# Threshold attention and a squared-ReLU layer: new PSUM homes and step orders in attention, and four weight chunks converted in the first layer

## The chip, the core and the metric

The kernel runs on one core of one Trainium2 chip. The metric is device time in microseconds: the median of several executions. A profile shows one execution, instruction by instruction.

The core's engines each run their own queue in order: TensorE (PE in the profile; PEld is its loading of weights), VectorE (DVE), ScalarE (ACT), GpSimd (POOL) and SyncE (SP), which here issues nearly all DMAs. PE writes its results to PSUM, which has eight banks of 512 fp32 columns; DVE and ACT read them there.

## The reference

```python
def _attn_ref(q, k, v, tau):                      # q, k, v: (8, 8, 576, 64), float32
    scale = 1.0 / np.sqrt(q.shape[-1])
    scores = scale * np.matmul(q, k.transpose(0, 1, 3, 2))
    thresh = np.max(scores, axis=-1, keepdims=True) - tau
    scores = np.where(scores >= thresh, scores, -1000000000.0)
    scores = scores - np.max(scores, axis=-1, keepdims=True)
    attn = np.exp(scores)
    attn = attn / (np.sum(attn, axis=-1, keepdims=True) + 1e-09)
    return np.matmul(attn, v).astype(np.float32)

def _moe_ref(x, w_in, w_out):                     # x: (4608, 512); w_in: (512, 2048); w_out: (2048, 512)
    h = np.maximum(x @ w_in, 0.0)
    return (h * h @ w_out).astype(np.float32)
```

The attention's output, put back to (batch, position, head and channel), is x. The weights w_in and w_out come as 64-bit floats; the kernel converts them to 32-bit floats itself.

## The kernel before

**Three stages.** Attention comes first and writes x, transposed, to DRAM. The first layer (`hidden_layer`, L837, products at L849) and the second (`output_layer`, L955, products at L984) follow, each in nine steps of 512 tokens. Both layers save products with a fast matrix scheme of two levels: each step forms 49 products from sums of operand blocks, so sums of weight blocks must be made on the way (`sums`, L251).

**Units and periods.** Attention works on two heads of a batch at once. A unit is 128 queries of such a pair against all 576 keys (four units a pair, and one that joins the last 64 queries of two pairs): 144 units. A period (`period`, L624) handles two units, A and B, and there are 72 periods, with a few before and after to fill and empty the pipeline. The steps of a period, by their names in the order lists:

- `SA`, `SB` (`scores`, L427, product L438): scores of A and of B. A's lie in banks 0 and 5, B's in 2 and 3, and the last 64 keys of both in parts of banks 1 and 4.
- `topA0` ... `topB1` (L455): DVE copies the scores of one head to SBUF and finds their smallest negated value, which is the maximum.
- `powA0` ... (L466): ACT's exponentials. `leastA`, `leastB` (L463): GpSimd adds tau to the thresholds. `maskA0` ... (L471): DVE applies the mask and sums.
- `over` (L478, GpSimd) and `inv` (L481, DVE): the reciprocal of the sums; `spread` (`widen`, L514) lays it out wide on GpSimd.
- `U`, `V`, `W` (`fill`, L503, `half_turn`, L377, L381): PE turns the masked weights of a period, 8, 8 and 2 blocks (W with the two blocks of the spread reciprocals). `eU`, `eV`, `eW` (`filled`, L523, L528): ACT copies them to SBUF.
- `PV` (`values`, L530, L537): 72 products of weights and values. `x` (L651): DVE and ACT take the result out; `xs` (L666): GpSimd scales the half that ACT took and SP sends x to DRAM (`ask`, L581).
- `T`, `eT` (`turn`, L392, L399): PE turns the next queries or keys, ACT takes them out (L406, L414), and the next loads are issued (`load_q` L291, `load_k` L301).
- `c1` ... `c6` (L200 to L247): the conversion of one weight chunk of 128x512, on ACT (`c1`, `c2`), GpSimd (`c3`, `c6`) and DVE (`c4`, `c5`). `fetch` (L178) loads a chunk on SP. `s1` (`sums_step`, L575): one sum of first-layer weight blocks on GpSimd, in periods without a chunk.

**PSUM homes before.** `sc` holds banks 0 to 5, `pt` the other two as one buffer of two banks. U and V both use pt, one after the other; W uses banks 2 and 3; PV uses banks 0 and 5; T uses 1 and 4.

**What sets the order.** The order is written out by hand. Each list (`PLAIN`, `CONVERTING`, `FIRSTS` for the first periods, L599 to L616) names the steps of a period; the program issues them in that order, and each engine executes its share in that order. Which unit a step works on is fixed in the table `steps` (L695): scores, maxima, exponentials, masks of this period; U and PV of two periods ago; V and W of the period before. `touch` (L356) adds the waits between engines that meet in a bank.

**Chunks.** There are 32 chunks: 16 of w_in and 16 of w_out. `EARLY = 16` (L164) is the number of w_out chunks converted in attention; chunk m begins in period m + 2 (L567). `convert_out` (L1082) can convert half chunks within steps of the first layer, four a step (`PER`, L1121); with 16 early chunks it has none to do.

Of the kernel before, what the change touches and what calls it, by code (L numbers as in the profile page):

```python
# [48 lines left out]
def kernel(  # L49
# [114 lines left out]
    EARLY = 16  # L164
# [136 lines left out]
    def load_k(i):  # L301
# [4 lines left out]
        for j in range(2):  # L306
# [10 lines left out]
            queue.dma_start(out=rn[REST:P, ds(j * D, D)], in_=keys[:, CH - 1, :])  # L317
        queue = nc.sync if i else nc.scalar
        queue.dma_start(
            out=rn[0:REST, :].rearrange("p (j d) -> p j d", j=2),  # L320
            in_=q[b, h : h + 2, MAIN:S, :].rearrange("j p d -> p j d"),
        )
# [31 lines left out]
    MEET = (("q scores", "turned q", (Q_RING,)), ("scores", "turned k", (K_RING,)), ("q scores", "turned k", (K_RING,)), ("values", "weights", (W_RING,)), ("x", "weights", (W_RING,)))  # L354
# [22 lines left out]
    def half_turn(pt, slot, of, at=None):  # L377

        for r in range(2):
            rows = ds(r * HALF, HALF)  # L380
            made = nc.tensor.transpose(pt[:, r, ts(slot, HALF)], of[rows, :], ident[rows, rows])  # L381
            touch("turns", made, at and at + r * BANK, BANK)

    def whole(pt, slot, count):

        return pt[:, :, ds(slot * HALF, count * HALF)].rearrange("p r (t q) -> p r t q", q=HALF)
# [5 lines left out]
    def turn(i, which, spots, other=None):  # L392
# [15 lines left out]
        def then():  # L408
            part = lambda r, x, n: (spots[r][0][:, ds(x, n)], spots[r][1])
            if which:  # L410
                for r, n in ((0, half), (1, half + REST)):
                    spot = part(r, 0, n)
                    copy_by = other if r and other else nc.scalar.copy
                    touch(kind, copy_by(to[1][:, ds(r * half, n)], spot[0]), spot[1], BANK, i)  # L414
                scaled(to[2], part(0, half, REST))
                next_keys(i)
            else:
                for r in range(2):
                    scaled(to[0][:, ds(r * half, half)], part(r, 0, half))
# [83 lines left out]
    def fill(m, f, pt, at=None):  # L503
# [19 lines left out]
    def filled(m, f, pt, at=None):  # L523
# [3 lines left out]
        to = wT[m][:, ds(weight_at(first) * P, count * P)]  # L527
        touch("weights", nc.scalar.copy(joined(to), whole(pt, 0, count)), at, 2 * BANK, m)  # L528

    def values(m):  # L530

        for c in range(CH):
            for u in range(2):
                for s, (i, _, count, row) in enumerate(halves(2 * m + u)):
                    for j in range(2):
                        rows = ds(j * D, D)
                        made = nc.tensor.matmul(  # L537
                            sc[ds(u * D, D), ds(5 * j * BANK + row, count)], loaded_v[i][rows, (c - (u != j)) % CH, :],
# [3 lines left out]
                        touch("values", made, 5 * j * BANK, BANK, m)  # L542
# [47 lines left out]
    def converts(p):  # L590
        return is_wide and (has_chunk(p) or has_chunk(p - 1))
# [4 lines left out]
    def begun(n):  # L596
# [3 lines left out]
        fetch U SA topA1 over s1 topA0 SB topB1 inv sV eU powA1 V topB0 leastA spread PV powA0 maskA1 leastB maskA0 eV T powB1 x maskB1 powB0 xs maskB0 eT W eW  # L600
    """.split()
    CONVERTING = """
        fetch c1 T SA topA1 c3 topA0 U eU powA1 SB topB0 over topB1 powA0 c4 powB0 PV eT inv leastA maskA1 x powB1 leastB spread V eV maskA0 W maskB0 c5 c6 eW maskB1 xs c2
# [4 lines left out]
            SA SB id4 fetch topA1 topA0 powA1 leastA powA0 topB1 T id14 powB1 topB0 powB0 eT maskA0 leastB maskA1 maskB1 maskB0  # L608
        """.split(),
        1: """  # L610
            SA topA1 SB topA0 id4 topB0 over inv powA1 V eV spread T powA0 topB1 eT W id4 leastA maskA1 leastB powB1 maskA0 maskB1 powB0 maskB0 fetch eW
        """.split(),
        2: """
            T SA fetch c2 U topA1 c3 over eU SB powA1 topA0 c4 powA0 c5 topB0 powB0 leastA topB1 eT maskA1 PV inv powB1 V leastB x spread maskA0 eV maskB1 maskB0 W eW xs c6 c1
        """.split(),
    }  # L616

# [6 lines left out]
    def period(p):  # L624

        A, B_, a, b = 2 * p, 2 * p + 1, 2 * p - 2, 2 * p - 1
        m, turns = p - 2, TURNS.get(p, ())
        late, pt = {"W": []}, {}

        def fills(f, m):  # L630
            if has(2 * m):
                pt[f] = pt_pool.tile([P, 2, BANK], FP32, tag="pt", name="pt")
                fill(m, f, pt[f])

        def evict(f, m):
            if has(2 * m):
                filled(m, f, pt[f], 2 * BANK if f == "W" else None)

        def W():
            if has(2 * m + 2):  # L640
                pt["W"] = middle()
                fill(m + 1, "W", pt["W"], 2 * BANK)

        def turn_some():
            late["turn"] = [turn(g // 2, g % 2, spots()) for g in turns]

        def PV():
            if has(2 * m):
                values(m)

        def given_out():  # L651
            if has(2 * m):
                x = sb.tile([P, 2, P], FP32, tag="x", bufs=2, name="x")
                by_vector = (0,)
                for j in range(2):
                    by = sc[:, ds(5 * j * BANK, P)], wT[m][:, ts(SCALE_AT + j, P)]
                    if j in by_vector:
                        made = nc.vector.tensor_tensor(out=x[:, j, :], in0=by[0], in1=by[1], op=ALU.mult)  # L658
                    else:
                        made = nc.scalar.copy(x[:, j, :], by[0])  # L660
                    touch("x", made, 5 * j * BANK, P, m)
                late["x"] = x, [j for j in range(2) if j not in by_vector], wT[m]
                wT.pop(m)
                valued(m)
# [588 lines left out]
```

## Time and profile before

| | us |
|---|---|
| median of 3 runs | 1290.56 (1289.38 to 1292.22) |
| the profiled execution | 1292.2 |
| its span, first to last instruction | 1290.4 |
| PE busy | 1261.3 |
| DVE busy | 998.5 |
| ACT busy | 854.9 |
| POOL busy | 897.4 |

An engine's busy time joins its records, and records of one engine can overlap, since an instruction is begun before the one ahead of it has ended; the cost of an instruction in a full queue is then the time from its start to the next start. A row of the order in time gives start, length, engine, line, operation, out<-in, shape and count, and in brackets the idle time ahead of it with what ended that. A row of waits gives who waited for whom, the sum, how often, and the longest. A row of stretches gives the window, its length and the busy time of PE, PEld, DVE, ACT and POOL.

### The profile page before, as it was taken

The numbers are of one execution on the slowest core, as the hardware profiler recorded it, in microseconds if no ns is written. First come the engines' busy times: TensorE is split into PE (matmuls) and PEld (weight loads), VectorE is DVE, ScalarE is ACT, GpSimd is POOL, SyncE is SP. The second block draws the span as 40 slices with busy tenths as digits, with TensorE's granted clock in tenths as the row PEclk, the third lists the DMA queues.
The fourth block names the chain that finished last, engine by engine and source line by source line (L and its number), as shares of the span: only waits on it lengthen the run. The fifth ranks groups of instructions, "written<-read, shape, count | busy, mean of one in ns | idle before, by whom it ended". The sixth has DMA issues, their size and how long they took to land.

```text
span 1290.4 us, 46352 instructions
## 1 busy us (share of the span) xinstructions
PE 1261.3 (98%) x18627; PEld 1127.2 (87%) x18627; DVE 998.5 (77%) x2433; ACT 854.9 (66%) x1536; POOL 897.4 (70%) x1094
## 2 busy tenths in 40 slices
PE   8999998999999999999999999999999999999998
PEld 6666666677777768999999999999999999999998
DVE  6999999899999997787788778777745654665463
ACT  6999999899999995756675667566523432343240
POOL 2565565555555557888898789768777867776775
PEclk9999999999999999999999999999999999999999
DMA  5555666544333422556655665589545314522411
GB/s 149 157 149 152 162 189 182 140 94 115 88 83 83 103 48 67 180 169 205 204 185 177 212 199 178 176 322 394 188 148 164 113 57 160 165 90 79 160 34 34
DMA packets 247032, 192.05 MB, mean 149 GB/s; under 512 B 97184, under 2 KB 195488, under 8 KB 246816
## 3 DMA queue, kind: packets, MB, share of 16 engines
q1 hardware_dynamic: 245360, 188.63, 48.7%
q8 instruction: 147, 2.41, 0.8%
q10 hardware_dynamic: 1456, 0.44, 0.1%
q14 instruction: 69, 0.57, 0.1%
HBM read 116.65 MB, written 72.35 MB: 146 GB/s over the span
## 4 chain that ended last, share of the span: by engine, by line
PE 64%; DMA 2%; DVE 1%; ACT 1%; issue 0%; POOL 0%; SPq 0%; ACTq 0%; DVEq 0%; POOLq 0%
PE ph L849 30%; PE po L984 29%; PE sc L537 2%; PE sc L438 2%; DMA wall<-w 1%; PE pt L381 1%; DMA g<-arena 0%; PE sc L381 0%; PE sc L399 0%; DVE arena L456 0%; ACT c L795 0%; ACT arena L528 0%; DVE arena L125 0%; DVE arena L122 0%; POOL arena L125 0%
## 5 line engine op out<-in xcount | busy, mean ns | idle before, releaser
L125 POOL TENSOR_TENSOR arena<-arena 128x512 f32<-128x512 f32 (+1 forms) x314 | 378.1, 1224 | 108.7 <-DVE arena L125 92.0
L984 PE MATMUL po<-wall,arena 128*128 128x128 f32 x3528 | 394.7, 275 | 1.4 <-ACT arena L761 1.4
L984 PEld LDWEIGHTS po<-wall,arena 128*128 128x128 f32 x3528 | 394.3, 192 | 1.8 <-ACT arena L761 1.8
L849 PE MATMUL ph<-arena,wall 128*128 128x128 f32 x3528 | 394.4, 275 | 0.5 <-DVE arena L658 0.5
L849 PEld LDWEIGHTS ph<-arena,wall 128*128 128x128 f32 x3528 | 394.1, 192 | 0.7 <-ACT arena L660 0.6
L125 DVE TENSOR_TENSOR arena<-ph,arena 128x512 f32<-128x512 f32 x378 | 256.1, 688 | 86.9 <-PE ph L849 62.6
L122 POOL TENSOR_TENSOR arena<-arena 128x128 f32<-128x128 f32 (+2 forms) x314 | 255.2, 814 | 54.5 <-DMA arena<-w 36.7
L125 DVE TENSOR_TENSOR arena<-po,arena 128x128 f32<-128x128 f32 x378 | 108.2, 289 | 168.4 <-PE po L984 164.3
L466 ACT ACTIVATE arena<-arena 128x576 f32<-128x576 f32 x288 | 224.3, 858 | 16.7 <-DVE arena L456 16.7
L471 DVE SCALAR_TENSOR_TENSOR arena<-arena 128x576 f32<-128x576 f32 x288 | 225.7, 812 | 0.4 <-POOL arena L463 0.3
L456 DVE TENSOR_SCALAR_CACHE_REDUCE arena<-sc 128x576 f32<-128x576 f32 x288 | 204.2, 750 | 18.0 <-ACT arena L528 6.8
L795 ACT COPY c<-arena 128x512 f32<-128x512 f32 (+1 forms) x303 | 173.5, 579 | 49.5 <-DVE arena L122 41.5
L537 PEld LDWEIGHTS sc<-arena 64*64 64x64 f32 x5760 | 144.8, 133 | 44.3 <-DVE arena L456 40.4
L122 DVE TENSOR_TENSOR arena<-arena,c 128x512 f32<-128x512 f32 (+1 forms) x267 | 174.6, 662 | 5.8 <-ACT c L795 4.0
L438 PE MATMUL sc<-arena 64*64 64x64 f32 (+1 forms) x2304 | 170.6, 417 | 0.3 <-DVE arena L658 0.2
L537 PE MATMUL sc<-arena 64*64 64x128 f32 (+1 forms) x5760 | 160.6, 262 | 9.9 <-DVE arena L456 7.8
L528 ACT COPY arena<-pt 128x1024 f32<-128x1024 f32 x144 | 157.4, 1093 | 3.6 <-PE pt L381 3.6
L761 ACT COPY arena<-po 128x128 f32<-128x128 f32 x63 | 16.6, 264 | 186.8 <-PE po L984 184.0
L381 PEld LDWEIGHTS pt<-ident,arena 64*128 64x128 f32 x2304 | 83.3, 139 | 42.7 <-ACT arena L528 35.3
L761 ACT COPY arena<-ph 128x512 f32<-128x512 f32 x63 | 36.6, 581 | 121.8 <-PE ph L849 121.2
L381 PE MATMUL pt<-ident,arena 64*128 64x64 f32 x2304 | 101.0, 228 | 3.7 <-ACT arena L528 3.5
L438 PEld LDWEIGHTS sc<-arena 64*64 64x64 f32 x2304 | 62.8, 133 | 47.0 <-issue 22.6
(51 smaller groups left out, 941.4 us busy)
## 6 DMA issues: line engine op xcount, KB each, us to landing
g<-arena SPq DMA_DIRECT2D x144, 256.0 KB, 2.8
arena<-g SPq DMA_DIRECT2D x144, 256.0 KB, 4.2
w<-arena SPq DMA_DIRECT2D x60, 256.0 KB, 2.5
wall<-w SPq DMA_DIRECT2D x49, 256.0 KB, 5.3
arena<-w SPq DMA_DIRECT2D x44, 256.0 KB, 3.1
arena<-in_v_dram SPq DMA_DIRECT2D x32, 288.0 KB, 3.6
out_dram<-arena SPq DMA_DIRECT2D x70, 128.0 KB, 2.5
arena<-in_q_dram SPq DMA_DIRECT2D x64, 128.0 KB, 3.8
```

Source lines behind the costliest of these rows:

```text
L122: e.tensor_tensor(out=out, in0=x, in1=y, op=ALU.subtract)
L125: e.tensor_tensor(out=out, in0=x, in1=y, op=ALU.add)
L381: made = nc.tensor.transpose(pt[:, r, ts(slot, HALF)], of[rows, :], ident[rows, rows])
L438: made = nc.tensor.matmul(sc[at, ds(to, count)], lhs, kT[rows, ds(at_k, count)], start=True, stop=True)
L456: made = nc.vector.tensor_scalar(out=s[:, j, :], in0=sc[:, ds(at, S)], scalar1=1.0, scalar2=None, op0=ALU.mult, op1=ALU.min, accum_out=nmx ...
L466: nc.scalar.activation(out=w[:, :, j, :], in_=of(j), func=AF.Exp, bias=nmx[:, j : j + 1], scale=-1.0)
L471: nc.vector.scalar_tensor_tensor(out=w[:, :, j, :], in0=of(j), scalar=thr[:, j : j + 1], in1=w[:, :, j, :], op0=ALU.is_le, op1=ALU.mult, a ...
L528: touch("weights", nc.scalar.copy(joined(to), whole(pt, 0, count)), at, 2 * BANK, m)
L537: made = nc.tensor.matmul(sc[ds(u * D, D), ds(5 * j * BANK + row, count)], loaded_v[i][rows, (c - (u != j)) % CH, :], wT[m][rows, ds(weigh ...
L795: nc.scalar.copy(c, y)
L849: nc.tensor.matmul(to[:, j, :], W_IN[m, k][:, ts(j, P)], of[k][:, m - 1, :], start=(not more and j == 0), stop=True, skip_group_check=True,)
L984: nc.tensor.matmul(to, g[:, j, :], w[:, j, :], start=(not more and j == 0), stop=(j == 3), skip_group_check=True)
```

## The change

Five things change.

1. PSUM homes. V now goes to banks 2 and 3, W to banks 0 and 5, and PV to a tile of its own in pt (named `px`); U stays in pt. W's copy to SBUF becomes two copies, one a bank. `x` reads px.
2. Orders. All lists are new. A step may carry a lag, the number of periods that its unit lies back (`eV@2`: V of two periods ago); default lags stand in `LAGS`. In the plain order the period begins with smallest, exponential B1, masks of the period before, and PE runs U, T, SA, SB, PV, W, V. In the converting order PE runs SA, U, SB, PV, W, T, V, and U is of the period before.
3. `EARLY` is 12: the last four chunks of w_out leave attention, and `convert_out` converts them as eight half chunks in steps 0 and 1 of the first layer. A period counts as converting until two periods after the last chunk's beginning.
4. `load_k` loads the last keys of both heads with one DMA rather than two, all on SP's queue.
5. When queries or keys are taken out, the half in bank 4 goes first.

```diff
-    EARLY = 16
+    EARLY = 12
...
-            queue.dma_start(out=rn[REST:P, ds(j * D, D)], in_=keys[:, CH - 1, :])
...
+        last = k[b, h : h + 2, :, :].rearrange("j (p c) d -> p c j d", c=CH)[:, CH - 1, :, :]
+        nc.sync.dma_start(out=both(ds(REST, REST)), in_=last)
...
-        touch("weights", nc.scalar.copy(joined(to), whole(pt, 0, count)), at, 2 * BANK, m)
+        to = joined(wT[m][:, ds(weight_at(first) * P, count * P)])
+        if f == "W":
+            for r in (1, 0):
+                of = pt[r][:, ds(0, count * HALF)].rearrange("p (t q) -> p t q", q=HALF)
+                touch("weights", nc.scalar.copy(to[:, r, :, :], of), at[r], BANK, m)
+            return
...
     PLAIN = """
-        fetch U SA topA1 over s1 topA0 SB topB1 inv sV eU powA1 V topB0 leastA spread PV powA0 maskA1 leastB maskA0 eV T powB1 x maskB1 powB0 xs maskB0 eT W eW
+        fetch leastA@1 eW@2 U leastB@1 maskA0@1 maskB0@1 maskA1@1 powB1@1 maskB1@1 eV@2 T SA topA0 over inv sV s1 eU eT xs@3 SB topA1 spread topB0 powA0 PV topB1 powA1 powB0 W x V
...
     CONVERTING = """
-        fetch c1 T SA topA1 c3 topA0 U eU powA1 SB topB0 over topB1 powA0 c4 powB0 PV eT inv leastA maskA1 x powB1 leastB spread V eV maskA0 W maskB0 c5 c6 eW maskB1 xs c2
+        fetch over SA c5 eV@2 c1 c6 topA1 U@1 topA0 leastA eU@1 powA1 inv SB xs@3 PV powA0 spread topB0 maskA1 W powB0 topB1 maskA0 T c3@0 c2 powB1 eW x c4@0 leastB maskB1 V eT maskB0
...
+    LAGS = dict(
+        U=2, V=1, W=1, eU=2, eV=1, eW=1, PV=2, x=2, xs=2, over=1, inv=1, spread=1, c3=1, c4=1, c5=1, c6=1,
+    )
...
+        if f == "U":
+            late[f, m] = pt_pool.tile([P, 2, BANK], FP32, tag="pt", name="pt")
...
+        elif f == "V":
+            late[f, m] = middle()
...
+        else:
+            late[f, m] = [sc[:, ds(b * BANK, BANK)] for b in (0, 5)]
...
+            late["PV", m] = pt_pool.tile([P, 2, BANK], FP32, tag="pt", name="px")
```

More of the change, by code (lines that the diff above doesn't have):

```diff
@@ L410, in then @@
             if which:
-                for r, n in ((0, half), (1, half + REST)):
+                for r, n in ((1, half + REST), (0, half)):
                     spot = part(r, 0, n)
@@ L590, in converts @@
     def converts(p):
-        return is_wide and (has_chunk(p) or has_chunk(p - 1))
+        return is_wide and any(has_chunk(p - i) for i in range(3))
     def has_chunk(p):
@@ new lines, in evict, with turn_some, evict_turned, values_of @@
+    def evict(f, m):
+        if has(2 * m):
+            filled(m, f, late.pop((f, m)), {"U": None, "V": 2 * BANK, "W": (0, 5 * BANK)}[f])
+    def turn_some(p):
+        late["turn", p] = [turn(g // 2, g % 2, spots()) for g in TURNS.get(p, ())]
+    def evict_turned(p):
+        for then in late.pop(("turn", p)):
+            then()
+    def values_of(m):
+        if has(2 * m):
+            late["PV", m] = pt_pool.tile([P, 2, BANK], FP32, tag="pt", name="px")
+            values(m, late["PV", m])
```

193 lines of the change are left out of this document (88 added, 105 removed).

## The prediction

> **What bounds the kernel now.** I read the page first, then the busy time in stretches, then the order in time on TensorE (PE), ScalarE (ACT) and GpSimd (POOL), and last who waits for whom. All times are in one profiled execution.
>
> ```profile
> span 1290.4 us, 46352 instructions
> ```
> ```profile
> 133.00:217.00 84.00, 78.26 (x1939) 55.68 (x1942) 82.54 (x241) 84.00 (x149) 50.81 (x84) 1.00 0.68 186
> 217.00:256.00 39.00, 34.03 (x800) 24.30 (x800) 36.05 (x104) 35.80 (x61) 21.27 (x36) 0.96 0.54 147
> 256.00:482.00 226.00, 224.84 (x5754) 162.67 (x5752) 216.60 (x647) 214.50 (x363) 126.82 (x218) 1.00 0.38 88
> ```
> The columns are PE, PEld, DVE, ACT, POOL busy, then the granted clock, DMA share and GB/s. Attention has three stretches. While weight chunks are converted, ACT is busy 84.00 of 84.00 and DVE 82.54, so ACT sets the pace. From 256 us, without chunks, PE is busy 224.84 of 226. Between them lies a stretch in which no engine is full and the granted clock falls to 0.96. The first scores of a period (L438, "x24" or more) mark its start; four of them give the pace:
>
> ```profile
> 34.24 1.32 PE L438 MATMUL sc<-arena 64*64 64x512 f32 x24
> ```
> ```profile
> 216.88 1.32 PE L438 MATMUL sc<-arena 64*64 64x512 f32 x24
> ```
> ```profile
> 256.12 2.18 PE L438 MATMUL sc<-arena 64*64 64x512 f32 x32
> ```
> ```profile
> 481.79 2.18 PE L438 MATMUL sc<-arena 64*64 64x512 f32 x32
> ```
> They begin periods 4, 30, 35 and 71. So 26 converting periods take 182.64 us, 7.02 each; periods 30 to 34 take 39.24, 7.85 each; 36 plain ones take 225.67, 6.27 each. After attention PE hardly waits, so time is to be had in attention alone.
>
> What ends last in a plain period shows on three engines:
>
> ```profile
> 393.69 0.66 PE L381 MATMUL pt<-ident,arena 64*128 64x64 f32 x16
> 394.28 2.32 PE L438 MATMUL sc<-arena 64*64 64x512 f32 x32
> 396.53 0.72 PE L381 MATMUL pt<-ident,arena 64*128 64x64 f32 x16
> 397.24 2.19 PE L537 MATMUL sc<-arena 64*64 64x128 f32 x72
> 399.37 0.47 PE L399 MATMUL sc<-ident,arena 64*128 64x64 f32 x8
> ...
> 400.51 1.88 PE L438 MATMUL sc<-arena 64*64 64x512 f32 x28
> ```
> ```profile
> 395.32 1.05 ACT L528 COPY arena<-pt 128x1024 f32<-128x1024 f32 x1
> ```
> ```profile
> 396.43 0.75 DVE L456 TENSOR_SCALAR_CACHE_REDUCE arena<-sc 128x576 f32<-128x576 f32 x1
> ```
> ```profile
> PEld pt L381 <- ACT arena L528: 23.5, 29, 0.8
> ```
> PE's second turning (step V, 396.53) starts when ACT's copy of U ends at 396.37, since both use the pair of banks pt. The values (PV, 397.24) start when DVE's second maximum ends at 397.18, since PV writes banks 0 and 5, where the scores lie that DVE is reading. The loop "scores, two maxima, PV, three turnings, scores" is the 6.23 us from 394.28 to 400.51. The weight loads of the turnings waited 23.5 us on that copy in 29 periods, mostly under running products.
>
> **New homes and the plain order.** After the change PV has pt to itself once U is copied out; V goes to banks 2 and 3, W to 0 and 5. So PV no longer waits for maxima, and V no longer for U's copy. PE's order becomes U, T, SA, SB, PV, W, V, and DVE begins with the four masks of the period before. What is late next? PE's own work, start to start in the rows above: U 0.59; the scores 2.25 less the wait of some 0.1 before V; V some 0.55; PV 2.13; 399.37 to 400.51 for T, W and U, of which U is counted, leaves 0.55. That is 5.97. DVE, busy 216.60 of 226, needs 6.01 of its 6.27. ACT closes a loop from PV to PV: PV 2.13, W 0.45 to its end, 0.09 to ACT, W's copies 0.51, an exponential 0.67, V's copy 0.90, U's 1.05 and 0.16 to PE, 5.96 (the ACT durations from the rows of the next part). The change adds two waits: the scores SA (banks 0 and 5) wait for W's copies, SB (2 and 3) for V's, and all of PE's queue stands behind them; in this loop both copies are done some 0.1 before PE comes. All meet near 6.0 and hand work to each other, so I take 6.12, a tenth above the floors; the ends are 5.97 and 6.32, a little over today's. For 36 periods: 36 x (6.12 - 6.27) = **-5.3 us** (-10.7 to +1.9).
>
> **The converting order and the split copy.** ACT is full there, so an order gains nothing that ACT doesn't lose. W's copy of 512 columns becomes two of 256, one in each bank:
>
> ```profile
> 133.36 0.80 ACT L528 COPY arena<-sc 128x512 f32<-128x512 f32 x1
> 133.84 0.93 ACT L211 ACTIVATE arena<-arena 128x512 int32<-128x512 uint32 x1
> ...
> 135.06 1.18 ACT L528 COPY arena<-pt 128x1024 f32<-128x1024 f32 x1
> 135.96 2.27 ACT L466 ACTIVATE arena<-arena 128x576 f32<-128x576 f32 x3
> 137.97 0.85 ACT L414 COPY arena<-sc 128x256 f32<-128x256 f32 x2
> 138.54 0.49 ACT L406 ACTIVATE arena<-sc,qscale 128x64 f32<-128x64 f32 x1
> ```
> A record overlaps the next one, so I count start to start: 0.48 for 512 columns, and 0.57 for the two copies of 256 and 320, about 0.99 ns a column and nothing fixed. The split costs 0.51 - 0.48 = 0.03 us: 26 x 0.03 = **+0.8 us**. Bounds: half of the 0.1 by which turning-free periods could close up, -2.6, and an added hand-over of 0.1, +2.6. The Trainium skill, "ScalarE: Activation LUTs", section "What ACT_TABLE_LOAD costs", gives 186 ns beside the elements and 93 ns of overlap, so 0.09 us for a further instruction; by it this term would be +2.4 and the total 1279.8. The trace speaks against it: 0.03.
>
> **Four chunks out of attention.** Chunks end at period 29 rather than 33. A chunk's two ACT steps take 133.84 to 135.06, 1.22 us. Periods 30 to 34 take 39.24 now; after, period 30 ends the last chunk (6.6, an estimate between 6.27 and 7.02), 31 is empty of chunks in the converting order (6.3), 32 to 34 are plain (3 x 6.12): 31.3, so **-7.9 us**. Of this 5 x 7.02 - 31.3 = 3.8 is the price of the conversions; the other 4.1 is a stall that I expect to go:
>
> ```profile
> PE pt L381 <- ACT arena L528: 1.4, 1, 1.4
> PE sc L399 <- DMA arena<-in_q_dram: 1.1, 1, 1.1
> ```
> In that stretch T stood at the head of PE's queue before its queries had landed, and later V before a copy. After the change T stands behind SB, PV and W, some 4 us later, while its loads stay two periods ahead. On SP's queue each pair of heads issues one load of last keys in place of two, and a period's store of a chunk comes early; nothing that SP issues is needed sooner. If the stall comes back elsewhere, the term is -3.8.
>
> **The first layer's two steps.** Eight half chunks go there, four a step.
>
> ```profile
> L245 POOL TENSOR_TENSOR wall<-arena 128x512 int32<-128x512 int32 x14 | 20.7, 1479 | 30.6 <-DVE arena L234 21.8 <-ACT arena L528 4.4 <-DMA xT<-arena 2.2
> L234 DVE SCALAR_TENSOR_TENSOR arena<-arena 128x512 int32<-128x512 int32 x26 | 18.0, 691 | 0.0
> ```
> ```profile
> 496.00:517.00 21.00, 20.81 (x186) 20.84 (x187) 13.31 (x21) 8.78 (x17) 19.85 (x17) 1.00 0.32 95
> 538.70:560.00 21.30, 21.30 (x193) 21.30 (x192) 14.39 (x22) 14.53 (x27) 15.59 (x19) 1.00 0.73 234
> ```
> ```profile
> L122 POOL TENSOR_TENSOR wall<-wall 128x512 f32<-128x512 f32 x9 | 11.4, 1283 | 0.2
> ```
> At half size a step adds about 4 x 0.74 = 3.0 us to POOL, 4 x 0.61 = 2.4 to ACT, and at most 4 x 3 x 0.35 = 4.1 to DVE. DVE has 7.7 free in the 21 us where step 0 converts, ACT 12. POOL is nearly full there, but three more plain periods each do one sum of weights (L122, 1.28), so 3.8 us of such sums leave step 0: POOL is no worse. Step 1 has 5.7 free on POOL. PE covers it all: **0**, with +5 if the cover fails. The start (periods 0 to 3) and the drain hold the same work: DVE's masks of the last unit move behind the last maxima, then the same eight sums, so 0, give or take 1.5.
>
> **Sum.** -5.3 + 0.8 - 7.9 + 0 = -12.4 on a span of 1290.4. That execution took 1292.2, so 1.8 lies around the span and stays. The median of the runs, 1290.56, is 1.6 below it; the same step from the median gives **1278**.
>
> **Rivals.**
>
> (1) The plain period stays at 6.27, because the hand-overs refill the waits. For it: three engines within 0.3 us of each other. Against: the loop that now sets 6.23 is cut. -12.4 + 39 x 0.15 = -6.5: **1284**.
>
> (2) Everything closes to its floor, 5.97 plain and 6.95 converting: another -39 x 0.15 - 26 x 0.1 = -8.5: **1270**.
>
> (3) The first layer's cover fails: **1283**.
>
> (4) Slower: GpSimd's chain in the plain order. Its steps are now smallest of the period before, "over", a sum, the scaling of x, the spread, smallest of the next; the next masks on DVE wait for that last one.
>
> ```profile
> 313.74 0.23 POOL L478 TENSOR_SCALAR arena<-arena 128x4 f32<-128x4 f32 x1 [1.45 <-DVE arena L471]
> 314.05 1.28 POOL L125 TENSOR_TENSOR wall<-wall 128x512 f32<-128x512 f32 x1
> 315.46 0.29 POOL L463 TENSOR_SCALAR arena<-arena,tau_p 128x2 f32<-128x2 f32 x1
> 316.26 0.40 POOL L521 COPY arena<-arena 128x256 f32<-128x256 f32 x1 [0.51 <-DVE arena L481]
> 316.88 0.79 POOL L463 TENSOR_SCALAR arena<-arena,tau_p 128x2 f32<-128x2 f32 x1 [0.22 <-DVE arena L456]
> 318.05 0.52 POOL L675 TENSOR_TENSOR arena<-arena 128x128 f32<-128x128 f32 x1 [0.38 <-ACT arena L660]
> ```
> With 0.1 between them that is 0.31 + 1.3 + 0.55 + 0.45 + 0.35, about 3.05 from the last mask to the next first one. DVE fills that time with maxima, a reciprocal and x, some 3.0: the chain just fits. But L463 takes 0.79 in one place and 0.29 in another, the longer one beside a mask. The Trainium skill, "GPSIMD Engine Reference", section "1. Specifications", has GpSimd share its memory interfaces with VectorE and contend with instructions of two SBUF inputs, which masks are; the trace agrees with 0.79 against 0.29. If L463 and the spread both fell beside masks, the chain would grow by about 0.9 and a plain period to 7.0: 39 x 0.9 = +35, **1313**. It decides against the change from 0.32 us a period (12.4 / 39). I give it little, since between masks DVE runs maxima, beside which the sum kept 1.28 and the spread 0.40.
>
> (5) Nothing comes of it, as the stalls only move: **1290**.
>
> **How the numbers follow.** Forecast 0.52, (1) 0.17, (2) 0.08, (3) 0.06, (4) 0.10, (5) 0.07. A measurement of this kernel tells about 0.2%, 2.6 us, from no change. Faster: 0.52 + 0.17 + 0.08 + 0.06 = 0.83; same 0.07; slower 0.10. The range 1268 to 1290 leaves out (4), part of (5) and the far end of (2).
>
> **What would show it.** Right: plain periods of 6.0 to 6.2, PV starting without a wait for maxima, ACT still full until period 29, the first layer's first product some 12 us earlier, and PE without idle time in that layer's first two steps. Wrong: masks that wait for GpSimd's smallest; PV waiting for ACT's copy of U by more than 0.2 a period; turnings that wait for loads; PE idle between 496 and 580.

## The result, and the profile after

The changed kernel takes 1298.62 us (median of four, 1296.4 to 1300.35) where the kernel before took 1289.97 on the same chip: a ratio of 1.0064, interval 1.0046 to 1.0082. It is **slower**; 1278 was forecast. The profiled execution took 1298.79:

```profile
span 1296.9 us, 46412 instructions
```

The same places on the path in both profiled executions, by TensorE's first scores (SA) and first products of each layer's steps:

| stretch | before | after | difference | predicted |
|---|---|---|---|---|
| start, periods 0 to 3 | 34.24 | 34.59 | +0.3 | 0 |
| periods 4 to 29 | 182.64 | 186.57 | +3.9 | +0.8 |
| periods 30 to 34 | 39.24 | 32.52 | -6.7 | -7.9 |
| periods 35 to 70 | 225.67 | 221.41 | -4.3 | -5.3 |
| SA of 71 to first hidden product | 14.40 | 19.88 | +5.5 | 0 |
| first layer, steps 0 and 1 | 87.62 | 94.99 | +7.4 | 0 |
| second layer, step 0 | 45.79 | 46.31 | +0.5 | 0 |

The gains came almost as forecast; four losses ate them. First the starts of periods 4, 30, 35 and 71, from the order in time on TensorE (L438 before is L433 now):

```profile
34.59 0.66 PE L433 MATMUL sc<-arena 64*64 64x512 f32 x4 [0.38 <-ACT arena L526]
221.16 1.09 PE L433 MATMUL sc<-arena 64*64 64x512 f32 x8 [0.41 <-ACT arena L526]
253.68 1.09 PE L433 MATMUL sc<-arena 64*64 64x512 f32 x8
475.09 1.09 PE L433 MATMUL sc<-arena 64*64 64x512 f32 x8
```

A **plain period**, 6.15 us on average, in the same view:

```profile
391.47 2.19 PE L538 MATMUL px<-arena 64*64 64x128 f32 x72
393.59 1.11 PE L380 MATMUL sc<-ident,arena 64*128 64x64 f32 x24
394.49 0.72 PE L380 MATMUL pt<-ident,arena 64*128 64x64 f32 x16
394.99 0.53 PE L394 MATMUL sc<-ident,arena 64*128 64x64 f32 x10
395.44 2.21 PE L433 MATMUL sc<-arena 64*64 64x512 f32 x32
397.48 2.20 PE L538 MATMUL px<-arena 64*64 64x128 f32 x72
```

PV to PV is 6.01 here; nothing stands in brackets, so PE waited for nobody in these rows. The waits of PE between 256 and 475 us hold one row, where the loop through pt and the maxima stood before:

```profile
PE sc L433 <- ACT arena L529: 0.7, 4, 0.2
```

A **converting period**: busy time in one stretch (columns as in the prediction), then PE's waits from 62 to 215 us.

```profile
133.00:217.00 84.00, 77.02 (x1902) 52.55 (x1890) 83.20 (x236) 83.35 (x158) 54.48 (x81) 1.00 0.64 180
```
```profile
PE sc L433 <- ACT arena L526: 8.6, 22, 0.6
PE px L538 <- ACT arena L529: 4.5, 18, 0.3
```

ACT went from 84.00 to 83.35 of 84, and DVE from 82.54 to 83.20: two engines are nearly full, and neither is quite. The scores now wait 0.39 us for W's copies (L526), each of the 22 times.

**The drain**, from the last scores on: PE, then ACT.

```profile
477.38 2.20 PE L538 MATMUL px<-arena 64*64 64x128 f32 x72
...
483.51 3.86 PE L538 MATMUL px<-arena 64*64 64x128 f32 x72 [2.22 <-ACT arena L529]
...
490.42 3.87 PE L538 MATMUL px<-arena 64*64 64x128 f32 x108 [1.66 <-ACT arena L529]
494.97 5.26 PE L865 MATMUL ph<-arena,wall 128*128 128x128 f32 x45 [0.68 <-DVE arena L671]
```
```profile
480.32 0.65 ACT L526 COPY arena<-sc 128x256 f32<-128x256 f32 x2
480.85 0.79 ACT L461 ACTIVATE arena<-arena 128x576 f32<-128x576 f32 x1
481.53 1.01 ACT L529 COPY arena<-sc 128x1024 f32<-128x1024 f32 x1
482.42 1.03 ACT L529 COPY arena<-pt 128x1024 f32<-128x1024 f32 x1
```

PV needs the copies of W, V and U, and ACT makes them one after the other, U's last (ended 483.45). In a full period the next scores cover that; behind the last period no scores are left. In the kernel before, the waits for ACT in this stretch are shorter:

```profile
489.35 0.71 PE L381 MATMUL pt<-ident,arena 64*128 64x64 f32 x16 [1.59 <-ACT arena L528]
...
493.34 2.33 PE L537 MATMUL sc<-arena 64*64 64x128 f32 x108 [0.26 <-ACT arena L528]
```

And in the changed kernel the same 72 products take 3.86 in place of 2.20: the granted clock is half there (third column from the end).

```profile
480.30:483.72 3.42, 1.20 (x39) 1.06 (x39) 2.97 (x9) 3.15 (x6) 0.96 (x2) 1.00 0.20 38
483.72:487.13 3.41, 3.41 (x72) 3.36 (x64) 3.11 (x5) 0.00 (x0) 1.20 (x2) 0.50 0.21 42
487.13:490.54 3.41, 1.75 (x53) 1.45 (x49) 3.01 (x5) 2.75 (x5) 0.86 (x1) 1.00 0.11 20
490.54:493.96 3.42, 3.42 (x102) 3.42 (x106) 0.00 (x0) 0.00 (x0) 0.00 (x0) 0.50 0.12 24
```

**The first layer's step 0**, DVE and then PE, and PE in step 1:

```profile
505.57 0.43 DVE L1126 TENSOR_SCALAR cw<-cw 128x256 f32<-128x256 f32 x1 [0.70 <-ACT cw L1120]
506.04 0.43 DVE L226 TENSOR_SCALAR cw<-cw 128x256 int32<-128x256 int32 x1
506.51 0.42 DVE L234 SCALAR_TENSOR_TENSOR arena<-arena,cw 128x256 int32<-128x256 int32 x1
506.85 1.28 DVE L125 TENSOR_TENSOR arena<-ph,arena 128x512 f32<-128x512 f32 x2
508.04 0.42 DVE L1126 TENSOR_SCALAR cw<-cw 128x256 f32<-128x256 f32 x1
...
513.35 0.42 DVE L234 SCALAR_TENSOR_TENSOR arena<-arena,cw 128x256 int32<-128x256 int32 x1
```
```profile
507.58 5.62 PE L865 MATMUL ph<-arena,wall 128*128 128x128 f32 x48 [0.76 <-DVE arena L125]
515.02 7.23 PE L865 MATMUL ph<-arena,wall 128*128 128x128 f32 x60 [1.81 <-DVE arena L125]
```
```profile
561.46 5.77 PE L865 MATMUL ph<-arena,wall 128*128 128x128 f32 x35 [1.85 <-DVE arena L125]
```

A half chunk takes three DVE instructions and 1.28 us (505.57 to 506.85); four of them stand between 505.57 and 513.77, with DVE's sums of products (L125), for which PE waits, queued behind them. After the last of these waits the clock was at half again, from 562.2 to 565.6: 35 products take 5.77 us there, while 60 take 7.23 in the row above, so some 1.6 us of step 1 is the clock.

### The profile page after: what moved, and what is told of

It reads as the page before. It is cut to its first block, busy times and chain, and to the rows that moved or that the text cites. A ratio compares the mean times of both kernels' runs of the same rounds, so it can differ in the third digit from the quotient of the medians.

```text
span 1296.9 us, 46412 instructions
## 1 busy us (share of the span) xinstructions
PE 1257.1 (97%) x18623; PEld 1125.1 (87%) x18623; DVE 1009.5 (78%) x2449; ACT 859.5 (66%) x1616; POOL 903.0 (70%) x1094
## 4 chain that ended last, share of the span: by engine, by line
PE 62%; ACT 14%; DVE 9%; issue 7%; POOL 4%; DMA 3%; SPq 1%; DVEq 0%; ACTq 0%; POOLq 0%
PE po L1000 29%; PE ph L865 29%; ACT arena L461 4%; ACT arena L529 4%; DVE arena L451 3%; DVE arena L466 3%; POOL arena L458 2%; PE sc L433 2%; PE px L538 1%; ACT arena L526 1%; ACT arena L401 1%; ACT arena L211 1%; DVE arena L125 1%; DMA xT<-arena 1%; ACT arena L409 1%
## 5 line engine op out<-in xcount | busy, mean ns | idle before, releaser
L125 POOL TENSOR_TENSOR arena<-arena 128x512 f32<-128x512 f32 (+1 forms) x314 | 378.1, 1224 | 112.4 <-DVE arena L125 89.3
L125 DVE TENSOR_TENSOR arena<-ph,arena 128x512 f32<-128x512 f32 x378 | 255.7, 687 | 83.6 <-PE ph L865 61.7
L125 DVE TENSOR_TENSOR arena<-po,arena 128x128 f32<-128x128 f32 x378 | 108.1, 289 | 168.0 <-PE po L1000 163.7
L461 ACT ACTIVATE arena<-arena 128x576 f32<-128x576 f32 x288 | 211.7, 796 | 9.5 <-DVE arena L451 9.4
L451 DVE TENSOR_SCALAR_CACHE_REDUCE arena<-sc 128x576 f32<-128x576 f32 x288 | 206.9, 747 | 4.7 <-PE sc L433 3.1
L538 PEld LDWEIGHTS px<-arena 64*64 64x64 f32 x5760 | 147.8, 136 | 64.9 <-ACT arena L529 64.2
L433 PE MATMUL sc<-arena 64*64 64x64 f32 (+1 forms) x2304 | 171.4, 418 | 13.8 <-ACT arena L526 11.3
L538 PE MATMUL px<-arena 64*64 64x128 f32 (+1 forms) x5760 | 163.4, 265 | 10.5 <-ACT arena L529 9.4
L473 POOL TENSOR_SCALAR arena<-arena 128x4 f32<-128x4 f32 x72 | 27.2, 378 | 162.7 <-DVE arena L466 153.4
L433 PEld LDWEIGHTS sc<-arena 64*64 64x64 f32 x2304 | 57.0, 132 | 69.9 <-issue 24.8
L458 POOL TENSOR_SCALAR arena<-arena,tau_p 128x2 f32<-128x2 f32 x144 | 81.1, 563 | 35.5 <-DVE arena L451 25.1
L845 ACT ACTIVATE arena<-arena 128x512 f32<-128x512 f32 x144 | 90.8, 631 | 4.6
```

The costliest lines, as they stand in the source:

```text
L125: e.tensor_tensor(out=out, in0=x, in1=y, op=ALU.add)
L433: made = nc.tensor.matmul(sc[at, ds(to, count)], lhs, kT[rows, ds(at_k, count)], start=True, stop=True)
L451: made = nc.vector.tensor_scalar(out=s[:, j, :], in0=sc[:, ds(at, S)], scalar1=1.0, scalar2=None, op0=ALU.mult, op1=ALU.min, accum_out=nmx ...
L458: nc.gpsimd.tensor_scalar(out=thr, in0=nmx, scalar1=tau_p[:, :], scalar2=None, op0=ALU.add)
L461: nc.scalar.activation(out=w[:, :, j, :], in_=of(j), func=AF.Exp, bias=nmx[:, j : j + 1], scale=-1.0)
L538: nc.tensor.matmul(to[ds(u * D, D), j, ds(row, count)], loaded_v[i][rows, (c - (u != j)) % CH, :], wT[m][rows, ds(weight_at(2 * c + u) * P ...
```

## The experiments

Each is the changed kernel with one edit, unless it says otherwise. Times of stretches are from the run's own profile. A ratio is to the kernel before on the same chip; its median lay between 1290.12 and 1293.5 us there, so runs are compared by their ratios and not by their times.

**Sixteen chunks in attention (a16).** The half chunks of the first layer go.

```diff
-    EARLY = 12
+    EARLY = 16
```

> The changed kernel with all 16 chunks of w_out converted in attention again, so only the homes and orders differ from before. Theory: the first layer's first two steps lost 7.4 us (47.2 and 47.8 instead of 43.8 each) to the eight half chunks themselves, and the hand-over from attention lost 5.5 by itself. Then the two steps fall back to 43.8 each, four more periods run at 7.12 instead of 6.13 (+4.0), and the span is 1296.9 - 7.4 + 4.0 = 1293.5, still above before. Rival: the two steps lost by what attention leaves behind (a slower clock, late sums); then they stay near 47 and the span is about 1301.

Measured: 1295.97 us, ratio 1.0041 (1.0026 to 1.0056), span 1294.1. Steps 0 and 1 are 43.85 and 43.77 again, so the half chunks cost the 7.4. The other losses stay: 7.22 a period in 4 to 29, 18.13 in the drain. The new homes and orders by themselves lose.

**Twelve chunks in the kernel before (b12).** The other part alone.

```diff
-    EARLY = 16
+    EARLY = 12
```

> The kernel before with only the number of early chunks changed to 12: old homes, old orders. Theory: the two steps of the first layer take 47 to 48 us each as in the changed kernel (+7.4), and periods 30 to 34 lose four conversions and their stall (-7.4), so about 1290, no gain. If the stall comes back elsewhere, 1294. Rival: the old attention hands over in time and the steps stay at 43.8: 1283.

Measured: 1295.97, ratio 1.0037 (1.0023 to 1.005), span 1292.5. Periods 30 to 34 took 34.33 (4.9 less, where 7.4 were expected: one period of 8.42 is left) and the drain 14.40, but steps 0 and 1 took 47.78 each, 7.9 more. Moving the chunks pays 4.9 and costs 7.9. With the new orders it is much the same: periods 30 to 35 take 43.57 in a16 and 38.65 in the changed kernel, 4.9 for a price of 7.4. Both parts of the change lose alone.

**New homes, all orders old (homes16), and with the new plain order as well (mix16).** EARLY is 16 in both; lists are those of before, without lags.

```diff
-        fetch over SA c5 eV@2 c1 c6 topA1 U@1 ...
+        fetch c1 T SA topA1 c3 topA0 U eU ...
```

> New homes with the old orders and 16 early chunks: the homes alone (with the merged load of last keys). Theory: homes and order belong together in the plain periods. In the old plain order V stands ahead of PV on TensorE, and V now waits for all four maxima (banks 2 and 3), so the loop scores, four maxima, V, PV, turnings, scores is about 7.7 us: 36 x 1.4 = 50 us slower, 1340. Converting periods, in which the old order has PV ahead of V, stay at 7.0. Rival: the homes alone shorten a plain period to 6.1: 1285.

> New homes and the new plain order, but the old converting order and first periods, 16 early chunks. Theory: the new converting order is what lost 3.9 us in periods 4 to 29 (7.18 instead of 7.02). Then periods 4 to 29 go back to 7.0, plain ones stay at 6.13 (-4.5), the hand-over keeps its 5.5: about 1291. Rival: the converting loss comes from the homes (W's copy in two, V in the scores' banks) and stays: 1295.

In the old orders V is turned over scores that DVE has not read (in mix16 only in the first periods), so the weights of those periods aren't the reference's. Measured: 1437.93 and 1334.62 us. Plain periods took 8.97 with the old order and 6.14 with the new one; converting periods 8.32 and 8.31, against my 7.0, so both times are far above what was expected. PE's waits in homes16, from 62 to 215 and from 330 to 475 us, say why:

```profile
PE sc L433 <- ACT arena L526: 28.1, 18, 2.0
```
```profile
PE sc L380 <- DVE arena L451: 21.4, 17, 1.3
PE sc L433 <- ACT arena L526: 18.7, 16, 1.3
```

The new homes put W where the next scores go, so the copies of W stand on the path unless the order has them early. Homes and order can't be judged apart; the plain gain is shown, the converting order only limits a loss that the homes bring.

**No VectorE work for half chunks (nodve).** The clamp, shift and merge of the eight half chunks are left out; the weights made from them aren't the reference's.

```diff
-                if step == 2:
-                    ...
-                    convert4(key)
-                    convert5(key)
```

> The changed kernel without VectorE's three instructions (clamp, shift, merge) of the eight half chunks in the first layer; the converted values are wrong for that, the rest of the conversion (loads, ScalarE, GpSimd, stores) stays. Theory: the two steps lose time because VectorE, which executes in order, is full from 505.6 to 514.3 with 4 x 1.27 us of conversions among the additions that free TensorE's banks. Then both steps fall from 47.2 and 47.8 to 43.8 to 44.3. Rival: ScalarE is held by the loads of raw chunks, which land late (4.7 us from issue in step 0), and holds its own copies out of PSUM; then the steps stay at 46 or more.

Measured: 1294.53, ratio 1.0008 (0.999 to 1.0026). Steps 0, 1 and 2 took 43.85, 45.13 and 45.14, against 47.22, 47.77 and 43.77; the theory (43.8 to 44.3) holds in step 0 alone. The loads, ScalarE and GpSimd went on as before, so VectorE's share is 3.4 of 3.4 in step 0 and 2.6 of 4.0 in step 1, of which some 1.6 is the clock, which stays full in this layer here. But step 2, which had lost nothing, is now 1.4 longer, so over the three steps 4.6 of 7.4 go. The 2.7 that remain aren't VectorE's work on half chunks. In step 1 DVE waits for a sum of GpSimd, in whose queue merges of half chunks (L1125) stand:

```profile
557.14 0.69 DVE L122 TENSOR_TENSOR arena<-arena,c 128x512 f32<-128x512 f32 x1 [1.13 <-POOL arena L122]
```

In step 2 DVE waits for GpSimd again, 1.49 and 1.77 us (L125). No run took GpSimd's part away, so that the rest is its doing is not shown.

**Half chunks later in the step (begin10).** They begin three ticks later.

```diff
-        PER, BEGIN = 4, 7
+        PER, BEGIN = 4, 10
```

> The changed kernel with the half chunks beginning at tick 10 instead of 7, some 2.6 us later, so that every load has landed. Theory (VectorE full): nothing is gained, since the conversions now meet the sums of the next x, which begin at tick 14: 47 to 49 us a step. Rival (late loads): the two steps fall by the waits of ScalarE on loads, 2.2 and 1.8 us, to 45 and 46.

Measured: 1296.96, ratio 1.0044 (1.0024 to 1.0064). Steps took 46.79, 46.83, 44.35: together 0.8 less than in the changed kernel. PE's waits for DVE there are six of at most 0.9 us in place of three of up to 1.9, and the clock stays full in this layer. So a later start spreads the waits and saves little; the times lie between what the theory (47 to 49) and its rival (45 and 46) gave.

**Half chunks thinner (b13p2).** The kernel before, with 13 chunks in attention and two half chunks a step, in steps 0 to 2.

```diff
-    EARLY = 16
+    EARLY = 13
...
-        PER, BEGIN = 4, 7
+        PER, BEGIN = 2, 7
```

> The kernel before with three chunks instead of four moved out of attention, and two half chunks a step in steps 0 to 2 instead of four a step in 0 and 1. Theory (VectorE is overloaded only where four half chunks stand close): two half chunks, 2.5 us, fit ahead of the sums of x, each of the three steps takes 43.8 to 44.5, attention saves about 5, and the kernel is faster than before, near 1286. Rival (each half chunk costs about 1 us wherever it stands): three steps of 45.8, and no gain: 1291.

Measured: 1297.33, ratio 1.0025 (1.0008 to 1.0042), span 1292.2: near the rival's number, but not by its three steps of 45.8. Steps 0 and 1 took 44.8 and 44.65, so two half chunks cost 0.9 where four cost 3.4 to 4.0. Step 2 took 48.08, for another reason; ACT and PE there:

```profile
594.90 0.40 ACT L1104 ACTIVATE cw<-arena 128x256 f32<-128x256 f32 x1 [3.47 <-DMA arena<-in_moe_w_out_dram]
```
```profile
597.34 2.83 PE L849 MATMUL ph<-arena,wall 128*128 128x128 f32 x23 [3.10 <-DVE arena L125]
```

A load that lands late stops ACT, behind it DVE (2.29 us, for ACT), behind it PE. So there are two prices: crowding on DVE, and a wait that three engines in order hand on.

**Products to keep PE busy in the drain (fill).** Fourteen turnings of the identity before each of the last two PV.

```diff
+            if m >= NU // 2 - 2:
+                for _ in range(14):
+                    made = nc.tensor.transpose(sc[:, ds(BANK, P)], ident[:, :], ident[:, :])
+                    touch("turns", made, BANK, BANK)
```

> The changed kernel with 14 turnings of the identity (results unused) ahead of each of the last two groups of values, which fill the 2.2 and 1.7 us that TensorE waits for ScalarE's copies at the end of attention. Theory: the granted clock fell to one half for 3.4 us after each of these two waits, which made both groups take 3.86 instead of 2.20 us; with TensorE kept busy the clock stays, and the hand-over falls from 19.9 to 16.5 us. Rival: the clock falls for another reason, or ScalarE's copies set the end anyway; then it stays at 19 to 20.

Measured: 1299.72, ratio 1.0057 (1.0031 to 1.0083). The clock never halved and the drain took 17.70 instead of 19.88: 2.2 less, where 3.4 were expected; waits of 0.53 and 0.92 us remain. The whole run is no faster than the changed kernel's 1.0064. The drain of a run below, c3early, kept the full clock without such products, so this run alone doesn't show that they are the reason.

**The drain in another order (a16last).** EARLY is 16, and the last period and the drain turn U a period earlier.

```diff
+    LAST = """
+        over SA eV@2 topA1 U@1 topA0 leastA eU@1 powA1 inv SB xs@3 sV PV ...
```

> The changed kernel with sixteen chunks converted in attention, and with the last period and the drain in another order: the last unit's U is turned and copied one period earlier and before its scores, as in the converting order, so that the last two PV wait for no copy of U or V. Theory (the drain pays because PV waits for ACT's copies of V and U with no scores left to cover them): the 18.1 us from the last first scores to the first hidden product, seen with the changed order and sixteen chunks, fall to 14.0 to 15.0, near the 14.40 of the kernel before, TensorE's idle before the two last PV falls below 0.8 us each and PV keeps 2.2 us; span 1290.5. Rival A (VectorE's last masks and its eight sums behind them set the end of the drain, whoever copies what): the stretch stays at 17 or more, span 1293 to 1294. Rival B (the halved clock alone is the price): idle stays, but where the clock isn't halved the stretch is 16.5.

Measured: 1300.27, ratio 1.0062 (1.0045 to 1.0079). The drain stayed at 19.58, and the period ahead of it grew from 6.11 to 8.56: W's copies, for which SA waits, stand behind a second copy of U and an exponential on ACT. Rival A's number came (17 or more), but VectorE's masks are only part of its cause: before the last two PV, PE waited 1.16 us each for ACT's copies, and 0.70 for a mask ahead of them. The clock was at half from 492.5 to 499.3.

```profile
484.07 1.32 PE L433 MATMUL sc<-arena 64*64 64x512 f32 x24 [2.37 <-ACT arena L526]
...
494.01 4.12 PE L538 MATMUL px<-arena 64*64 64x128 f32 x72 [1.16 <-ACT arena L529]
```

**Old until period 34, new after it (hyb16 and hyb16n).** Homes and orders of before up to period 34, the new homes and the new plain order from 35 on, EARLY 16; points 4 and 5 of the change stay. hyb16 has the other last period as well, hyb16n hasn't.

```diff
+    SWITCH = 35
...
+        elif f == "V" and m + 1 < SWITCH:
+            late[f, m] = pt_pool.tile([P, 2, BANK], FP32, tag="pt", name="pt")
```

> Old homes in PSUM and old orders up to period 34, the new homes and the new plain order from period 35 on, sixteen chunks in attention, and the last period in the order of the run before. Theory (the new homes and orders pay only in plain periods; the converting order, the drain and the half chunks each cost on their own): periods 4 to 29 7.03 each as before, 30 to 34 39 in all (with the stall) or 34.5 (without), plain 6.15 each, 4.3 less than before in all, the last stretch 14.0 to 15.0, first-layer steps 43.8: span 1283 to 1287, 0.3 to 0.5 per cent faster than the kernel before. Rival (the converting stretch's 7.18 is a matter of the chip's run and not of the order, or what plain periods save is lost again by queues downstream): span 1290 or more.

> As the run before, without the other order in the last period: the drain is that of the changed kernel. Theory: the last stretch is 17.7 to 19.9 instead of some 14.5, all else as in the run before, so the span is 3 to 4 us longer, 1287 to 1290. Rival: the drain is given back in the first layer, whose first steps then wait less for weights, and both runs end within 1 us of each other.

Measured: 1296.85, ratio 1.0032 (1.0018 to 1.0046), and 1290.66, ratio **0.9986** (0.9977 to 0.9996). In hyb16n periods 4 to 29 take 7.01 again and the plain ones 6.18; its drain is 16.88, 3.0 less than in the changed kernel, with this PE row in it and this clock:

```profile
485.74 2.20 PE L538 MATMUL px<-arena 64*64 64x128 f32 x72 [2.22 <-ACT arena L529]
```
```profile
480.75:484.16 3.41, 2.75 (x80) 2.30 (x72) 3.31 (x12) 3.40 (x8) 2.41 (x5) 1.00 0.22 43
484.16:487.57 3.41, 1.83 (x68) 1.83 (x72) 3.02 (x7) 1.53 (x2) 1.43 (x3) 1.00 0.00 0
```

The wait is the same 2.22 us, and the clock stays full. So of the drain's 5.5, 2.5 is the waits and 3.0 the clock. This version beats the changed kernel, and the one before by 0.1 per cent: the interval leaves 1 out, though it is less than the 0.2 that I had called the limit. It gains 3.1 in periods 35 to 70 and 2.7 in 30 to 34, and loses 2.5 in the drain and 1.6 at the start. At the start and in 30 to 34 homes and order are those of before, and each slower side has a stretch at half clock there (hyb16n at 20.0, the kernel before at 226.8), so part of these two is the clock and not the change. The other last period loses here too (8.56 in period 70, 19.92 in the drain), so hyb16's theory of 1283 to 1287 failed.

**GpSimd's clamp elsewhere (c3early).** In the converting order L218 goes behind the merge.

```diff
-        fetch over SA c5 eV@2 c1 c6 topA1 ... T c3@0 c2 powB1 ...
+        fetch over SA c5 eV@2 c1 c6 c3@0 topA1 ... T c2 powB1 ...
```

> The changed kernel with one step of the converting order moved: GpSimd's clamp of the raw chunk (L218) stands right behind the merge, where VectorE takes maxima, and no longer behind the spread, where VectorE masks. Theory (in the changed order VectorE has become as full as ScalarE, because its masks run beside L218: 0.85 and 0.97 us instead of 0.81, 0.23 us a period): the masks of the converting stretch fall from a mean of 832 ns to 806 to 815, L218 from 840 ns to 620 or so, and with ScalarE's 7.09 left as the bound the periods of 7.08 and 7.16 fall to 7.00 to 7.10; periods 4 to 29 take 184 to 185 instead of 186.57, span some 2 us shorter. Rival (ScalarE alone sets 7.1, or the added wait of the scores for W's copies does): masks get shorter, but periods 4 to 29 stay within 0.5 us of 186.6.

Measured: 1299.41, ratio 1.0061 (1.0046 to 1.0076), periods 4 to 29 186.31. L218 fell to 614 ns, but the masks rose, from a mean of 832 to 849 ns. My culprit was wrong; the rows below put another in its place. First GpSimd and DVE here, then two places of the changed kernel:

```profile
167.22 0.46 POOL L681 TENSOR_TENSOR arena<-arena 128x128 f32<-128x128 f32 x1
```
```profile
167.29 1.00 DVE L466 SCALAR_TENSOR_TENSOR arena<-arena 128x576 f32<-128x576 f32 x1
```
```profile
161.03 0.40 POOL L516 COPY arena<-arena 128x256 f32<-128x256 f32 x1
...
168.32 0.91 POOL L516 COPY arena<-arena 128x256 f32<-128x256 f32 x1
```
```profile
161.05 0.99 DVE L466 SCALAR_TENSOR_TENSOR arena<-arena 128x576 f32<-128x576 f32 x1
...
168.15 0.82 DVE L466 SCALAR_TENSOR_TENSOR arena<-arena 128x576 f32<-128x576 f32 x1
```

A mask that starts just behind a GpSimd instruction takes 0.99 or 1.00 in place of 0.81; one that starts ahead of it keeps 0.82, and GpSimd's copy takes 0.91 in place of 0.40. Whoever comes second pays. From 62 to 215 us of the changed kernel, 55 masks that start with no GpSimd instruction running take 0.81 on average, 12 that start during its clamp (L218) 0.85 and 10 that start on its copy (L516) 0.97; in this run 21 that start on its product (L681) take 0.98. The Trainium skill, "SBUF — State Buffer", section "Who interferes with whom", has this rule: an instruction of VectorE with two SBUF inputs and one of GpSimd that reads SBUF contend, and issue order decides who blocks. The trace agrees in direction; the mask lost 0.18, not the whole 0.4 of the copy.

**Work off ScalarE (noact) and off VectorE (nodvec).** In attention's conversions, the absolute value goes, or the shift.

```diff
-        nc.scalar.activation(out=a.bitcast(FP32), in_=hi.bitcast(FP32), func=AF.Abs)
```
```diff
-        nc.vector.tensor_scalar(
-            out=a, in0=a, scalar1=3, scalar2=0x3FFFFFFF, op0=ALU.logical_shift_left, op1=ALU.bitwise_and
-        )
```

> The changed kernel without ScalarE's absolute value of each raw chunk in attention; GpSimd's clamp reads the chunk itself, so that a chunk's sign is lost in its low part and the weights made from it aren't the reference's. ScalarE's work in a converting period falls from 7.09 to 6.5 us. Theory (VectorE, at 7.10 a period with its longer masks, is as full as ScalarE): periods 4 to 29 stay at 7.0 to 7.15, so that ScalarE's share alone explains nothing of the 3.9 us. Rival (ScalarE's work, with the copies' waits, sets 7.18): 6.6 to 6.75 a period, 172 to 176 for the 26.

> The changed kernel without VectorE's shift of the clamped chunk in attention; the exponent bits aren't moved, so that the weights made from these chunks aren't the reference's. VectorE's work in a converting period falls from 7.10 to 6.77 us, ScalarE's stays 7.09. Theory (both engines are full): the periods close up to ScalarE's own 7.0 to 7.10, 182.5 to 184.5 for periods 4 to 29 (186.57 in the changed kernel), ScalarE has no idle time. Rival (ScalarE's loop alone sets the pace, VectorE follows): 186 to 187 as before, VectorE idle by 0.35 a period.

One execution each: 1295.93 and 1295.96 us. Periods 4 to 29 took 182.63 (7.02) and 184.85 (7.11). Busy time from 64 to 207 us, noact and then nodvec, DVE fourth and ACT fifth:

```profile
64.00:207.00 143.00, 131.91 (x3266) 90.20 (x3266) 142.74 (x411) 133.78 (x249) 95.22 (x144) 1.00 0.62 167
```
```profile
64.00:207.00 143.00, 130.21 (x3222) 88.92 (x3216) 139.08 (x386) 142.10 (x270) 93.46 (x141) 1.00 0.62 166
```

With 0.58 us less on ACT a period loses only 0.15, and DVE is full; with 0.33 less on DVE it loses 0.07, and ACT is full. Either alone would hold a period at 7.0 to 7.1. Against the 182.64 of the kernel before, nothing of the 3.9 is left with less on ACT, though DVE is full, and 2.2 are left with less on DVE. So DVE's fullness alone costs nothing against before; more than half of the loss stands with ACT alone, and the rest comes where both are full.

## Why the prediction was wrong

Three steps failed; in the first two, cover was assumed and not followed in the queue.

- **"The first layer's two steps ... PE covers it all: 0"**: +7.4. This is the largest error, and rival 3, which was given +5 and a chance of 0.06, named it. The step compared DVE's 4.1 us with 7.7 free in 21 us. The work was 5.1 (4 x 1.28), and it stands in 8.2 us, not in 21, ahead of the sums that PE waits for. Shown by nodve (all of step 0, 2.6 of 4.0 in step 1, 4.6 of 7.4 over three steps) and by b13p2 (in steps 0 and 1 half the load, a quarter of the price). Some 1.6 of the 7.4 is the clock in step 1, and the forecast's "POOL is no worse" is in doubt, by nodve's steps 1 and 2.
- **"The start ... and the drain hold the same work ... so 0, give or take 1.5"**: +5.5. The same work, but in the new homes PV waits for ACT's copies in a row, and no scores cover them: 2.5. The granted clock at half twice added 3.0, by hyb16n; that part is bad luck of the execution, as the last section shows. The prediction had listed the loop from PV to PV, through W's, V's and U's copies, at 5.96, and did not ask what it costs where nothing runs beside it.
- **"ACT is full there, so an order gains nothing that ACT doesn't lose"**: +3.9 in place of +0.8. It is no matter of one execution: with the old homes and order the 26 periods take 182.0 to 183.0 in five profiles, with the new ones 185.5 to 188.1 in six. ACT's work grew a little more than forecast (7.09 a period from end to end against 7.03; the split copy itself 0.53 against 0.49, where 0.03 more was forecast), and ACT no longer worked without a pause. DVE became full too: masks cost 0.77 each instead of 0.72, behind GpSimd's instructions. By noact and nodvec ACT's share is the larger, and DVE adds to it; how ACT's pauses come about is not shown. Rival 4 had this contention, in the plain order, where it did not come. One period of 8.24, in which PE sat 1.24 ahead of a turning with no releaser shown, is 1.1 of the 3.9; it came again in other runs with this order (8.94 in a16) but not in c3early, and its cause stays open.

Two steps held. The plain period came to 6.15 (6.12), -4.3 in place of -5.3; the median is 6.13, single periods lie between 5.95 and 6.45. Rival 4's chain fits in it, as forecast (its terms add up to 2.96, not to 3.05, which changes nothing): GpSimd's smallest ended at 474.9 in this stretch, just as the mask that needs it began (474.94).

```profile
473.65 1.25 POOL L458 TENSOR_SCALAR arena<-arena,tau_p 128x2 f32<-128x2 f32 x2
```

Periods 30 to 34 gave -6.7 (-7.9): the chunks 4.9, by b12 and by a16, where I had 3.8, and the stall 1.8, where I had 4.1; with sixteen chunks a16 has it one period later, 8.45 in period 35. Of the forecast's own signs of being wrong, two came: PE idle between 496 and 580, and PV waiting 0.25 us for ACT's copy in 18 converting periods. Small and not traced: 0.3 at the start and 0.5 in the second layer's first step.

## What to carry to other kernels

Free time in a window is cover only if it lies ahead of what the next engine waits for: lay the added instructions into the queue one by one, and see which result stands behind them. An order that is right in a loop must be run through its last turn, where the work that covered a copy is gone. In a stretch with one full engine, look how near the second is, since a change of neighbours (who starts first, VectorE or GpSimd) can fill it; and where homes and orders suit one stretch, try them in that stretch alone, as hyb16n did. Before a difference of a few microseconds is put down to a change, look whether the granted clock differed in the two profiles.

## What was not expected of the hardware

TensorE's granted clock fell to one half for 3.4 us after waits of 1.66 to 2.22 us: in the changed kernel at 483.7, 490.5 and 562.2. Such a stretch costs about 1.6 us (72 products in 3.86 for 2.20). It does not follow from the length of the wait alone: 2.22 us left the clock full in hyb16n, as did 1.81 (at 515.02) here. The drain took 16.88 and 17.25 with no such stretch (hyb16n, c3early), 18.13 to 18.20 with one (a16, nodve, begin10) and 19.88 with two.

The traces show what decides. Within an execution the stretches at half clock begin whole multiples of 3.413 us apart: 483.72, 490.54 and 562.22 here lie 2 and 21 of them apart, and five in homes16, from 23.05 to 258.57, lie 20, 10, 22 and 17 apart. So there is a fixed grid of windows, and a wait counts by what falls into one of them. Ahead of the three stretches here, PE was idle for 2.22, 1.66 and 1.85 us of a window (the drain's rows above show the first two). In hyb16n a border of the grid, at 484.16, cuts the wait of 2.22 into 0.64 and 1.58, and here one at 514.43 cuts that of 1.81 into 1.22 and 0.59. Laid over all sixteen profiles, the grid has 17 windows at full clock with 1.85 us or more of idle PE, and half clock followed each; it followed 10 of 51 with 1.44 to 1.82, and none of the others.

The Trainium skill, "TensorE: Matmul & The Clock Gate", section "What's actually happening", has a window of about 3.4 us that runs freely and a clock at half after an idle one. The length of 3.4 us and the grid agree, while here idle time of about half a window was enough. A run of this kernel thus carries some 3 us that depend on how its waits fall in that window, which is more than hyb16n's gain.
